# Batched attention with a gated expert layer: narrowing v on GpSimd, block sums over 128 rows, a new rule for the constant products, weights and last rows in pieces

## The chip, the cores and the metric

The kernel runs on one core of a Trainium2 chip. The metric is the device time of one execution in microseconds. Every set of runs measured the kernel before beside the tested kernel on the same chip. Each run also lists its span (first to last instruction) and the mean clock that TensorE was granted. On one core a run is called slow when it is more than 1.5% above the fastest run of the same kernel.

## The reference, cut to what matters

```python
B, H, S, D = 4, 8, 768, 64          # q, k, v: fp32
k_sum = k.reshape(B, H, 24, 32, D).max(axis=3)     # one key per block of 32
v_sum = v.reshape(B, H, 24, 32, D).mean(axis=3)    # block sums of v (scaled)
# scores: 31 neighbours (|i-j| < 16) plus the 24 block keys, softmax, times [v, v_sum]
x = attn.transpose(0, 2, 1, 3).reshape(B, S, 512)
pooled = x.mean(axis=1)                            # the gate needs the whole batch
e_idx = argmax(pooled @ w_gate)                    # one of 8 experts per batch
out = gate_w * (relu(x @ w1[e_idx]) @ w2[e_idx])   # w1: 512x1024, w2: 1024x512
```

Two things follow for timing. The gate of a batch can only be computed when its attention is complete. And w1 and w2 (1 MB each in bf16, 2 MB as stored) cannot be loaded before the gate has named the expert.

## The kernel before: the parts that matter here

A list scheduler (class `Sched`) places every operation on its engine before the program is emitted. Where it thinks TensorE too idle, it inserts constant products, which compute nothing but keep TensorE active.

```python
SPAN = 3.0; DENSE = 0.47; FILL_TO = 50.0
def keep_warm(self, t, op):
    ...
    past = sum((e - max(s, t - self.SPAN)) * d for s, e, d in self.work[-40:] if ...)
    thin = self.DENSE * self.SPAN - past - n * unit
    if t > 7.0 and thin > 0:
        more = min(int(thin / unit) + 1, 10)
```

v arrives in fp32 in `v_f`. It is cast to bf16 straight into the place where the value products read it, in two halves of 64 rows. The block sums are products of those 64-row halves with a 0/1 selector `bind`: twelve for each of batches 1 to 3, and twelve smaller ones for each of the four pairs of heads in batch 0.

```python
def cast_v(b, c, eng):
    for odd in range(2):
        dst = vblks[b % 2][0:QB, c, odd:NJ:2, :, 0:D]
        src = v_f[odd * QB : (odd + 1) * QB, :, 2 * c : 2 * c + 2, :]
        ...
for j in range(NJ):                                   # NJ = 12
    nc.tensor.matmul(out_ps[p0 : p0 + 32, 0 : n * D], lhsT=bind[:, j, :],
                     rhs=vblks[b % 2][0:QB, ps, j, :, 0:D], ...)
```

w1 is loaded in two halves in batch 0 and whole in the others, on GpSimd's queue, behind the gate:

```python
def w1f(half):
    fs = slice(half * (F // 2), (half + 1) * (F // 2)) if b == 0 else slice(0, F)
    nc.gpsimd.dma_start(sb["w1"][:, :, fs], moe_w1[ds(sb["e"], 1)]...[:, :, fs])
```

The softmax here doesn't subtract the row's maximum and nothing guards it: scores larger than these inputs give would overflow.

## Time and profile before

| what | before |
|---|---|
| median of 3 runs | 183.13 us (181.32 to 185.94) |
| profiled run | 182.19 us, span 180.6, mean clock 0.941 |
| TensorE / VectorE / ScalarE / GpSimd busy | 95% / 57% / 61% / 27% |
| batch 0's gate (L839, first) | 43.81 us |
| first product of w1, batch 0 | 53.55 us |
| batch 3's gate | 143.52 us |
| TensorE at half clock | 22.72 to 43.2 us |

I divide the span into four stretches at three events that each kernel has: from the start to gate 0, from there to the first product with w1, from there to gate 3, and from there to the end. Before: 43.81, 9.74, 89.97 and 37.08 us. TensorE is nearly full, so what counts in each stretch is what TensorE has to do, at which clock, and what it waits for. The lines are shown in the prediction.

### The profile page before, as it was taken

How to read it: one execution, taken by the hardware profiler on the slowest of the kernel's cores; microseconds unless marked ns; L12 is line 12 of the kernel's file. 1: busy time of each engine (PE TensorE's matmuls, PEld its weight loads, DVE VectorE, ACT ScalarE, POOL GpSimd, SP SyncE). 2: the span in 40 equal slices, each digit the busy share in tenths (PEclk: the TensorE clock that was granted, in tenths of full speed). 3: DMA queues.
4: the chain of work that ended last, by engine and by line, in shares of the span. 5: the costliest groups of instructions: out<-in, count | busy, mean ns of one | idle time of the engine just before them, and what ended most of it. 6: DMA issues, size and time to landing. Idle time of an engine off the chain costs nothing.

```text
span 180.6 us, 4939 instructions
## 1 busy us (share of the span) xinstructions
PE 170.7 (95%) x2083; PEld 96.2 (53%) x2083; DVE 103.2 (57%) x240; ACT 110.3 (61%) x201; POOL 48.5 (27%) x70
## 2 busy tenths in 40 slices
PE   6988899999999999799999999999999999999991
PEld 2454756665646566354665654555575544465440
DVE  5899966546978766849893944089986200000000
ACT  3085244575887799244788873967899733377241
POOL 6999651000781160671026003000000030000000
PEclk9999955557999999999999999999999999999999
DMA  5999999705499999999999941999700049990063
GB/s 103 202 234 176 191 247 210 129 4 75 57 206 178 210 243 203 149 202 245 231 255 247 282 80 58 173 249 263 158 4 5 0 78 240 268 230 0 3 231 116
DMA packets 21590, 29.06 MB, mean 161 GB/s; under 512 B 3744, under 2 KB 15008, under 8 KB 21568
## 3 DMA queue, kind: packets, MB, share of 16 engines
q0 software_dynamic: 15184, 20.58, 64.4%
q1 hardware_dynamic: 6384, 8.17, 14.9%
q8 instruction: 16, 0.26, 0.6%
q14 instruction: 6, 0.05, 0.1%
HBM read 35.67 MB, written 6.29 MB: 232 GB/s over the span
## 4 chain that ended last, share of the span: by engine, by line
PE 63%; DMA 18%; DVE 10%; issue 3%; ACT 1%; POOL 1%; POOLq 1%; ACTq 0%; DVEq 0%
PE hps L949 12%; PE hps L980 12%; DMA q_nat<-in_q_dram 9%; PE third L949 6%; PE third L980 6%; DMA w_sb<-in_moe_w_dram 6%; DMA v_f<-in_v_dram 4%; PE sc L607 4%; PE ops L461 3%; PE ops L645 3%; PE tps L681 3%; PE third L1068 3%; DVE vblk L363 3%; PE kps L526 3%; PE tps L552 2%
## 5 line engine op out<-in xcount | busy, mean ns | idle before, releaser
L618 ACT ACTIVATE aT<-sc 128x768 bf16<-128x768 f32 x32 | 25.9, 810 | 14.4 <-PE sc L607 14.3
L949 PE MATMUL hps<-xT_b,w_sb 128*128 128x512 bf16 (+1 forms) x172 | 33.1, 328 | 0.4 <-DMA w_sb<-in_moe_w_dram 0.4
L262 POOL DMA_DIRECT2D v_f<-in_v_dram x30 | 25.2, 851 | 26.6 <-DMA w_sb<-in_moe_w_dram 11.6
L949 PEld LDWEIGHTS <-w_sb 128*128 128x128 bf16 x256 | 22.8, 98 | 14.2 <-DMA w_sb<-in_moe_w_dram 0.8
L980 PE MATMUL hps<-w_sb,hT_sb 128*128 128x512 bf16 x128 | 29.8, 380 | 0.0
L980 PEld LDWEIGHTS <-hT_sb 128*128 128x128 bf16 x192 | 17.8, 98 | 19.9
L1068 PE MATMUL third<-idle_in 128*128 128x512 bf16 (+2 forms) x79 | 22.4, 421 | 1.9 <-DVE warm L275 1.6
L960 ACT ACTIVATE hT_sb<-hps 128x512 bf16<-128x512 f32 (+1 forms) x43 | 20.6, 493 | 4.9 <-PE hps L949 4.7
L870 POOL DMA_DIRECT2D w_sb<-in_moe_w_dram x5 | 3.8, 760 | 70.4 <-PE third L980 32.6
L990 ACT ACTIVATE o_sb<-hps,gcol 128x512 f32<-128x512 f32 x16 | 11.0, 688 | 11.7 <-PE hps L980 8.3
L622 DVE TENSOR_TENSOR aT<-aT,mask 120x768 bf16<-120x768 bf16 x28 | 15.5, 556 | 3.0 <-ACT aT L618 2.6
L949 PE MATMUL third<-xT_b,w_sb 128*128 128x256 bf16 (+1 forms) x84 | 17.0, 325 | 0.0
L671 DVE TENSOR_TENSOR xs<-ops,rv 128x384 bf16<-128x384 f32 x28 | 15.6, 558 | 1.0
L546 DVE COPY kT<-kps 128x960 bf16<-128x960 bf16 (+1 forms) x20 | 14.1, 745 | 2.3 <-PE kps L526 2.3
L689 ACT ACTIVATE xT_b<-tps 128x768 bf16<-128x768 bf16 x16 | 12.9, 808 | 4.0 <-PE tps L681 3.9
L980 PE MATMUL third<-w_sb,hT_sb 128*128 128x512 bf16 x64 | 15.2, 380 | 0.0
L363 DVE CAST vblk<-v_f 64x768 bf16<-64x768 f32 x22 | 13.2, 601 | 2.4 <-issue 2.1
L1068 PEld LDWEIGHTS <-idle_in 128*128 128x128 bf16 x79 | 7.6, 111 | 11.9 <-issue 5.8
L645 PEld LDWEIGHTS <-aT 120*64 120x64 bf16 (+1 forms) x384 | 9.6, 119 | 7.9 <-issue 3.4
L461 PE MATMUL ops<-vblk,bind 64*32 64x128 bf16 (+1 forms) x84 | 12.0, 286 | 1.5 <-DVE vs L475 0.9
L990 ACT ACTIVATE o_sb<-third,gcol 128x512 f32<-128x512 f32 x8 | 5.5, 688 | 12.2 <-PE third L980 9.2
L361 ACT ACTIVATE vblk<-v_f 64x768 bf16<-64x768 f32 x10 | 8.5, 846 | 6.6 <-DMA v_f<-in_v_dram 6.6
(75 smaller groups left out, 207.1 us busy)
## 6 DMA issues: line engine op xcount, KB each, us to landing
w_sb<-in_moe_w_dram POOLq DMA_DIRECT2D x7, 1024.0 KB, 13.3
out_dram<-o_sb SPq DMA_DIRECT2D x24, 256.0 KB, 6.0
v_f<-in_v_dram POOLq DMA_DIRECT2D x30, 192.0 KB, 9.7
k_nat<-in_k_dram POOLq DMA_DIRECT2D x6, 384.0 KB, 8.9
q_nat<-in_q_dram POOLq DMA_DIRECT2D x6, 384.0 KB, 10.0
vblk<-vblk SPq DMA_DIRECT2D x12, 89.4 KB, 6.5
w_sb<-in_moe_w_dram POOLq DMA_DIRECT2D x2, 512.0 KB, 7.2
k_nat<-in_k_dram POOLq DMA_DIRECT2D x4, 192.0 KB, 4.5
```

Source lines behind the costliest of these rows:

```text
L262: eng.dma_start(v_f[:, :, h, :], v[b, h].rearrange("(j p) d -> p j d", p=128))
L363: eng.tensor_copy(dst, src)
L461: nc.tensor.matmul(out_ps[p0 : p0 + 32, 0 : n * D], lhsT=bind[:, j, :], rhs=vblks[b % 2][0:QB, ps, j, :, 0:D], start=(j == 0), stop=(j == ...
L618: nc.scalar.activation(aT, sb["sc"][:, :, 0 : NH * QB], ACT.Exp, scale=SCALE)
L622: nc.vector.tensor_tensor(out=aT[0:NR], in0=aT[0:NR], in1=mask[:, hf * NH : (hf + 1) * NH, :] .rearrange("p j c -> p (j c)") .unsqueeze(1) ...
L645: nc.tensor.matmul(ops[(j % 2) * QB : (j % 2 + 1) * QB, hh, jj // 2, :], lhsT=aT[0:rows, hh, jj * QB : (jj + 1) * QB], rhs=vb[0:rows, pr, ...
L671: nc.vector.tensor_tensor(out=sb["xs"][pr][:, hf * NS : (hf + 1) * NS, :, :].rearrange("p s h d -> p h s d"), in0=ops[:, :, :, 0:D], in1=r ...
L949: nc.tensor.matmul(ps["t"][:, 0 : c1 - c0], lhsT=sb["w1"][:, dt, ft * 128 : (ft + 1) * 128], rhs=sb["xT"][:, dt, c0:c1], start=(dt == 0), ...
L960: nc.scalar.activation(sb["hT"][:, ft, c0:c1], ps["t"][:, 0 : c1 - c0], ACT.Relu)
L980: nc.tensor.matmul(ps["t"], lhsT=sb["hT"][:, ft, st * 128 : (st + 1) * 128], rhs=sb["w2"][:, ft, :], start=(ft == 0), stop=(ft == NFT - 1),)
L990: nc.scalar.activation(ps["o"], ps["t"], ACT.Copy, scale=sb["gcol"][:, 0:1])
L1068: nc.tensor.matmul(idle[:, 0:c], lhsT=idle_in[:, 0:128], rhs=idle_in[:, 0:c], start=True, stop=True)
```

## The change

The intent is fourfold. Constant products follow a new rule of the scheduler: each kind of product gets a weight, and the scheduler asks for a mean of 1.05 over 3.4 us (`DENSE`, `SPAN`). These are numbers of the program. For batches 1 to 3, GpSimd narrows v to bf16 (`v_h`), so that VectorE's and ScalarE's copies into place read bf16 and the fp32 buffer comes free early. The block sums read `v_h` in 128 rows, six products instead of twelve. w1 comes in four pieces in batch 0 and in two in batch 3, and the last 128 output rows in two halves of columns. The tables that assign work to engines and the priorities were retuned with it.

```diff
-    DENSE = 0.47
+    DENSE = 1.05
...
-            thin = self.DENSE * self.SPAN - past - n * unit
+            thin = self.DENSE * self.SPAN - past - 2.5 * n * unit
...
-    CAST = ("DADD", "DDAD", "ADDD", "ADDA")
-    MK = ("DDPP", "DDDD", "DDDD", "DDDD")
+    CAST = ("AADA", "DDAD", "ADDD", "AADA")
+    CHUNKS = (4, 1, 1, 2)
+    MK = ("DDPP", "DDDD", "DDDD", "PDDD")
...
-            src = v_f[odd * QB : (odd + 1) * QB, :, 2 * c : 2 * c + 2, :]
+            src = (v_hs[b % 2] if b else v_f)[odd * QB : (odd + 1) * QB, :, 2 * c : 2 * c + 2, :]
...
+        for c in range(NP * (b > 0)):
+            narrow.append(add("POOL", 0.8, [loads[2 * c], loads[2 * c + 1]] + v_h_free.get(b - 2, []),
+                lambda b=b, hs=hs: nc.gpsimd.tensor_copy(v_hs[b % 2][:, :, hs, :], v_f[:, :, hs, :])))
...
+                for j in range(NH * (b > 0)):             # NH = 6
+                    nc.tensor.matmul(out_ps[p0 : p0 + 32, 0 : n * D], lhsT=bind2[:, j, :],
+                                     rhs=v_hs[b % 2][:, j, :, :], ...)
...
-            fs = slice(half * (F // 2), (half + 1) * (F // 2)) if b == 0 else slice(0, F)
+            fs = slice(c * F // CHUNKS[b], (c + 1) * F // CHUNKS[b])
...
+        return [o_st(st) for st in range(NST - 1)] + [
+            o_st(NST - 1, 0, DM // 2), o_st(NST - 1, DM // 2, DM) ]
```

(The list is cut; weights of single products, priorities and engine tables are left out.)

## The prediction

> **What bounds the kernel now.** I read the page first, then the timeline of TensorE, the busy time in short stretches, the chain and the groups. From the page:
>
> ```profile
> PE   6988899999999999799999999999999999999991
> DVE  5899966546978766849893944089986200000000
> PEclk9999955557999999999999999999999999999999
> DMA  5999999705499999999999941999700049990063
> ```
>
> TensorE is full nearly everywhere, so its own work sets the time, except in two places. First, slices 5 to 9 (22.6 to 45 us) run at half clock, with the DMA idle at the end: all loads are in, and the next weights wait for batch 0's gate (the expert's index). In stretches of one microsecond:
>
> ```profile
> 22.00:23.00 1.00, 1.00 (x43) 0.91 (x38) 0.99 (x1) 0.66 (x1) 0.59 (x1) 0.86 1.22 247
> 23.00:24.00 1.00, 1.00 (x17) 0.59 (x13) 1.00 (x3) 0.15 (x1) 0.24 (x1) 0.50 1.14 272
> ...
> 43.00:44.00 1.00, 1.00 (x12) 0.41 (x10) 0.00 (x0) 1.00 (x3) 0.00 (x0) 0.90 0.93 134
> ```
>
> The figure before the last two is the clock: it falls at about 22.72 us (0.86 = 0.72 x 1 + 0.28 x 0.5) and comes back near 43.2. What lay before each change, in the timeline (start, us, instructions):
>
> ```profile
> 19.09 0.39 PE L1068 MATMUL third<-idle_in 128*128 128x512 bf16 x1
> 20.05 0.86 PE L461 MATMUL ops<-vblk,bind 64*32 64x128 bf16 x12 [0.57 <-DVE vs L475]
> ...
> 39.44 2.00 PE L1068 MATMUL third<-idle_in 128*128 128x512 bf16 x5
> 41.23 0.85 PE L681 MATMUL tps<-identb,xs 128*128 128x128 bf16 x6
> 41.87 2.02 PE L1068 MATMUL third<-idle_in 128*128 128x512 bf16 x6
> 43.81 0.35 PE L839 MATMUL ops<-wg_sb,pooled 128*1 128x8 f32 x8
> ```
>
> L1068 are the constant products that only keep TensorE active. One of them in 3.5 us was too few; eleven in a row brought the clock back. L839, at 43.81, is batch 0's gate. The second place is the end:
>
> ```profile
> 153.26 2.21 PE L1068 MATMUL third<-idle_in 128*128 128x512 bf16 x10 [0.24 <-ACT o_sb L990]
> 155.86 1.90 PE L949 MATMUL hps<-xT_b,w_sb 128*128 128x512 bf16 x8 [0.39 <-DMA w_sb<-in_moe_w_dram]
> ```
>
> Batch 3's w1 was issued at 145.79 and landed 10.03 us later (the chain); TensorE ran out of batch 2's products at 153.02, so 2.84 us are lost. Between, TensorE idles little: 1.15 us at 73.5, where the gate's reciprocal sits on VectorE behind casts waiting for v.
>
> [...] The trace has no such copy; its selects on GpSimd took 287 ns for 128 columns and 591 for 384, 1.19 ns a column, so about 1.05 us for 768. [...] casts took 0.79 us while GpSimd issued loads (16.4 to 19.7) and 0.56 when it was idle (40.3).
>
> **The change part by part.**
>
> *Constant products.* The weights of the new rule, applied to the old trace with the windows laid from 22.72 backwards, give mean activities of 1.30, 1.58, 1.33 and then 0.86 (19.31 to 22.72) against the threshold of 1.05: it picks the window that lost the clock. The cold windows have 1.1 to 1.3, until 2.41 in the one that regained it. The compiled order shows for the changed kernel 38 units of 128 columns (18 and 20) around the second and third blocks' transposes, plus 13 before the last query transpose of batch 0. If the clock stays full, what ends batch 0's attention? In the 20.5 slow us TensorE's work is 10.3 at full clock, of which 3.1 are constant products, so VectorE, ScalarE and hand-offs take over. Adding VectorE's compiled instructions up to the gate at their old durations gives about 28 us (memsets 3.9, masks 2.3, key copies, maxima and query copies 8, normalisations 8 x 0.75, masks on scores 4 x 0.56, block sums 4 x 0.3, one pair of casts 1.2, three of batch 1 at 0.6, second memsets 1.6), start 1.1, so 29. It also gets lighter: two of three batch 0 pairs of casts go to ScalarE (2 x 1.2), which had 1 to 2 of 5 us busy there. With waits between score blocks (0.65 product + 0.81 exponential + two hand-offs, 1.8 us each, four in a row from about 20, then 5 us to the gate) I put the gate at 34 instead of 43.8.
> The loads limit this too: they keep the DMA full until 32 in the old trace, the narrowing of batch 1 needs v (landed near 30), and four copies (4.2 us) plus the new selector (two selects, 0.8) stand on GpSimd's queue before the gate's loads. So w1 goes out at about 36.5 instead of 46.3. Landing in quarters, its first products can start after some 5 us, at 41.5; TensorE's own list between gate and that point is about 6.9 us, the same time. Before: 53.5. Gain 12.0, of which 1.4 is the block sum of batch 1 and 0.6 two score products that move later.
>
> *Block sums.* From the groups:
>
> ```profile
> L461 PE MATMUL ops<-vblk,bind 64*32 64x512 bf16 x36 | 8.4, 378 | 0.0
> L363 DVE CAST vblk<-v_f 64x768 bf16<-64x768 f32 x22 | 13.2, 601 | 2.4 <-issue 2.1
> ```
>
> Twelve take 2.73 us in the chain, six of 128 rows half: 1.37 saved for each of batches 2 and 3, on the bound engine: 2.7.
>
> *Narrowing.* [...] v's buffer is free after GpSimd, not after the casts. Worth only the 1.15 us wait, half of which I count: 0.6.
>
> *Moved.* Batch 3's first pair masks by products: four of 384 columns, 0.32 to 0.38 us each at half clock (L596), so about 0.16 here: +0.6. The 0.6 of score products comes back.
>
> *End.* w1 in halves: 512 KB landed in 7.2 us (median of batch 0), so the first half is there 7.2 after issue instead of 10.0, when TensorE finishes its list: gain 2.8, less 0.5 because the output tiles of batch 2 still wait for stores (2.2 us twice on ScalarE). w2 landed near 162.4, 18.9 after the gate; needed 20 after it, so it just fits. Last rows in halves: the final eviction is 0.3 shorter, the store half as large: 0.5.
>
> Sum: 12.0 + 2.7 + 0.6 + 2.3 + 0.5 - 0.6 - 0.6 = 16.9 at best: span 180.6 to 163.7. The old profiled run is 182.2 us for that span, 1.6 more: 165.3.
>
> **The rivals.** (1) The clock falls in the changed kernel too. Its order from the last query transpose of batch 0 to the last value product has only three constant units. At full-clock durations of the trace times the rule's weights it holds four masked score blocks (0.60 us x 1.1), seven value products (0.58 x 0.66), three transposes of x (0.36 x 2.0), two transposes (0.46 x 1.35) and 0.4: 9.1 in all, from 8.6 us of TensorE. The hand-offs above stretch it to 11 to 13 us, which makes 0.70 to 0.83, under the 0.86 of the window that lost the clock. [...] I give this six chances in ten. It would come later than before (near 25) and meet less work: of the 17.9 us that the slow stretch from 25.98 to the gate takes now, half remains, 9 or so at half clock, so the gate comes at 37 to 38: 4 us back, 169.3. (2) The DMA becomes the bound. It is full from 46.3 to 106 in the old trace and moves earlier only by 9.8, while TensorE moves by 12 and more: stalls of 2 to 3 us before batch 2. Against it: some 12 us of idle DMA remain before and after. 168. (3) GpSimd is slow [...]: batch b's gate loads stand behind the copies of v of b+1, so w1 would come 3 to 4 us late three times. TensorE has 15 us of other products after gates 1 and 2, so mainly gate 0 pays: 169. (4) The clock part fails wholly: only 2.7 + 1.4 + 2.3 + 0.5 stay, 176.
>
> **Range and chances.** 165.3 plus 0.6 x 4 for rival 1, and some 1.3 for the lesser chances of rivals 2 and 3, gives 169.0 us. Low 163.5 is the sum with a fast state; high 176.5 is rival 4. The old three runs spread from 181.3 to 185.9[...]. Over 2% faster means under 179.5: all rivals but two at once give that, so 0.95; within 2% 0.04; slower 0.01.
>
> **What would show it.** Right: PEclk 9 in all slices of batch 0, or at most two of half clock; L839 first at 33 to 36; first product of w1 near 42; block sums of later batches 1.36 us; copies on GpSimd about 1.05 us; no constant products near the end, and under 1 us idle there. Wrong: half clock for 15 us or more; gates' loads on GpSimd waiting for narrowing; TensorE idle on w1 in the middle.

## The result, and the profile after

The changed kernel took 169.62 us (median of four runs, 168.70 to 171.37), the kernel before beside it 182.22 us. The ratio is 0.941, with a 95% interval of 0.923 to 0.959. Here and below, a ratio is the mean time of one kernel's fast runs over that of the other's of the same rounds, so it is not quite the ratio of the medians.

The profiled run is the slowest of the four: 171.37 us, span 169.8, clock 0.98, called slow. The page of the changed kernel, in 40 slices of 4.2 us:

```profile
PE   6989999799999997699999999999999999899992
DVE  5987985867997756977965746649754210000000
PEclk9999999969999999879999999999999999999999
DMA  4999999954999999699999989999200039994143
```

The five slices at half clock have become parts of three: in slice 8, and in slices 16 and 17. The DMA's hole, at slice 8 in both, is smaller. Stretches of one microsecond give the edges (the clock is the third figure from the right):

```profile
32.00:33.00 1.00, 0.92 (x26) 0.81 (x26) 0.61 (x2) 0.99 (x2) 0.00 (x0) 1.00 1.27 202
33.00:34.00 1.00, 0.93 (x3) 0.37 (x3) 0.84 (x4) 0.20 (x1) 0.91 (x2) 0.66 1.23 214
...
36.00:37.00 1.00, 1.00 (x4) 0.40 (x3) 0.23 (x1) 0.43 (x2) 0.00 (x0) 0.64 0.73 106
37.00:38.00 1.00, 1.00 (x34) 0.73 (x33) 0.36 (x4) 0.00 (x0) 0.00 (x0) 1.00 0.55 86
```

0.66 = 0.31 x 1 + 0.69 x 0.5: half clock from 33.31 to 36.72, for 3.41 us. A second such stretch lies at 70.86 to 74.27, also 3.41 us and 37.55 after the first, 11.0 times its length; the one of the kernel before (22.72 to 43.20, 20.48 us) is 6.0 times as long. Below, a window is a stretch of 3.41 us. In TensorE's timeline around the first (start, us, instructions, idle before):

```profile
30.59 0.35 PE L675 MATMUL ops<-vblk,aT 96*64 96x65 bf16 x10
31.81 0.22 PE L675 MATMUL ops<-vblk,aT 96*64 96x65 bf16 x2 [0.86 <-issue]
...
33.07 1.67 PE L1106 MATMUL third<-idle_in 128*128 128x512 bf16 x4 [0.16 <-issue]
34.54 0.85 PE L711 MATMUL tps<-identb,xs 128*128 128x128 bf16 x6
35.17 2.12 PE L1106 MATMUL third<-idle_in 128*128 128x512 bf16 x6
37.23 0.34 PE L869 MATMUL ops<-wg_sb,pooled 128*1 128x8 f32 x8
```

L675 are value products, L711 the transposes of x, L1106 the constant products, L869 the gate: at 37.23 instead of 43.81. Something new stands in the first lines: TensorE stops for 0.86 us in the middle of a group of twelve, waiting for nothing that the profile records ("issue"). Batch 1's gate is the second new thing. The timeline of all engines:

```profile
67.27 0.83 POOL L445 CAST v_h<-v_f 128x768 bf16<-128x768 f32 x1 [1.47 <-DMA v_f<-in_v_dram]
68.13 0.73 DVE L371 COPY vblk<-v_h 64x768 bf16<-64x768 bf16 x2 [1.18 <-POOL v_h L445]
68.50 0.75 POOL L899 DMA_DIRECT2D w_sb<-in_moe_w_dram  x1 [0.40 <-issue]
...
69.21 0.09 DVE L919 RECIPROCAL grec<-se 1x1 f32<-1x1 f32 x1
...
69.36 0.38 PE L922 MATMUL ops<-grec,ones_row 1*128 1x1 f32 x2 [1.26 <-DVE grec L919]
```

Read it backwards. TensorE waits 1.26 us for the gate's reciprocal. The reciprocal waits in VectorE's queue behind a copy into place (L371), that copy waits for GpSimd's narrowing (L445), and the narrowing waits for v to land. The load of w1 (L899) stands on GpSimd behind the same narrowing.

The end, where 2.84 us were lost before, now reads:

```profile
144.65 1.03 PE L980 MATMUL hps<-xT_b,w_sb 128*128 128x512 bf16 x4
145.51 0.60 PE L980 MATMUL third<-xT_b,w_sb 128*128 128x256 bf16 x4
146.64 1.02 PE L980 MATMUL third<-xT_b,w_sb 128*128 128x512 bf16 x4 [0.52 <-ACT hT_sb L991]
```

No constant products, 0.52 us of idle. And the groups of the parts that were exchanged:

```profile
L445 POOL CAST v_h<-v_f 128x768 bf16<-128x768 f32 x12 | 10.0, 831 | 8.5 <-DMA v_f<-in_v_dram 7.5 <-ACT hT_sb L991 1.0
...
L371 DVE COPY vblk<-v_h 64x768 bf16<-64x768 bf16 x14 | 5.8, 414 | 4.0 <-POOL v_h L445 3.8
L479 PE MATMUL ops<-v_h,bind 128*32 128x512 bf16 x18 | 5.4, 447 | 0.0
```

On average a narrowing takes 0.83 us and a copy into place 0.41 (before 0.60), and 18 sum products stand where 36 stood. The unaltered changed kernel was profiled twice more as a control, below. The last of these profiles is fast (169.49 us, span 167.9, clock 0.998), so it is the better partner of the profile of before. That one was fast in its own set of three, but it lies 2.0% above a later run beside it (178.68), and its clock of 0.941 is among the lower ones. By stretch, in us:

| kernel (profile) | to gate 0 | to first w1 product | to gate 3 | to the end | span |
|---|---|---|---|---|---|
| before | 43.81 | 9.74 | 89.97 | 37.08 | 180.6 |
| changed, first profile (clock 0.98) | 37.23 | 7.29 | 90.80 | 34.48 | 169.8 |
| changed, last control (clock 0.998) | 35.70 | 7.33 | 90.70 | 34.17 | 167.9 |

Batch 0 gave 9.0 to 10.5 us and the end 2.6 to 2.9. The middle, in which the block sums were halved, gave nothing: it is 0.7 to 0.8 us longer. That is what the experiments have to explain.

The runs also say how much of the gain goes with the clock. Three runs of the kernel before had a mean clock of 0.977 to 0.979 and took 176.57 to 177.68 us (mean 177.1). Seven runs of the changed kernel had 0.978 to 0.980 and took 171.09 to 173.66 us (mean 171.9). So about 5 of the 12.6 us between the medians remain at an equal mean clock; the rest goes with the clock. This is a comparison of runs and not a test.

### The profile page after: what moved, and what is told of

Its sections match the earlier page's. It is cut to its first block, busy times and chain, and to the rows that moved or that the text cites. A ratio compares the mean times of both kernels' runs of the same rounds, so it can differ in the third digit from the quotient of the medians.

```text
span 169.8 us, 4877 instructions
## 1 busy us (share of the span) xinstructions
PE 158.6 (93%) x2038; PEld 91.8 (54%) x2065; DVE 97.2 (57%) x232; ACT 112.1 (66%) x205; POOL 61.7 (36%) x87
## 4 chain that ended last, share of the span: by engine, by line
PE 69%; DMA 13%; POOL 8%; issue 4%; ACT 2%; DVE 1%; POOLq 1%; ACTq 0%
PE hps L1013 15%; PE hps L980 13%; PE third L1013 8%; DMA w_sb<-in_moe_w_dram 8%; PE third L980 6%; DMA v_f<-in_v_dram 5%; PE third L1106 4%; PE sc L637 4%; PE ops L675 3%; PE tps L711 3%; POOL v_f L263 3%; PE kps L556 3%; PE ops L479 2%; PE tps L582 2%; PE ops L487 2%
## 5 line engine op out<-in xcount | busy, mean ns | idle before, releaser
L980 PE MATMUL hps<-xT_b,w_sb 128*128 128x256 bf16 (+1 forms) x165 | 32.7, 326 | 0.6 <-issue 0.2
L1013 PE MATMUL hps<-w_sb,hT_sb 128*128 128x512 bf16 (+1 forms) x120 | 28.2, 373 | 0.5 <-issue 0.2
L899 POOL DMA_DIRECT2D w_sb<-in_moe_w_dram x8 | 6.0, 753 | 40.8 <-DVE grec L919 39.8
L1106 PE MATMUL third<-idle_in 128*128 128x512 bf16 (+3 forms) x61 | 18.8, 424 | 2.1 <-DVE warm L277 1.7
L1023 ACT ACTIVATE o_sb<-hps,gcol 128x512 f32<-128x512 f32 (+1 forms) x16 | 10.8, 674 | 10.0 <-PE hps L1013 6.6
L1013 PE MATMUL third<-w_sb,hT_sb 128*128 128x512 bf16 (+1 forms) x69 | 15.7, 367 | 0.3 <-issue 0.2
L1023 ACT ACTIVATE o_sb<-third,gcol 128x512 f32<-128x512 f32 (+1 forms) x9 | 6.0, 663 | 11.3 <-PE third L1013 4.6
L675 PEld LDWEIGHTS <-aT 120*64 120x64 bf16 (+1 forms) x384 | 8.7, 111 | 8.6 <-issue 3.7
L445 POOL CAST v_h<-v_f 128x768 bf16<-128x768 f32 x12 | 10.0, 831 | 8.5 <-DMA v_f<-in_v_dram 7.5
L700 DVE RECIPROCAL rv<-ops 128x6 f32<-128x6 f32 x28 | 5.4, 193 | 12.6 <-PE ops L675 10.2
L1106 PEld LDWEIGHTS <-idle_in 128*128 128x128 bf16 x67 | 6.6, 111 | 9.7 <-issue 4.1
L675 PE MATMUL ops<-vblk,aT 120*64 120x65 bf16 (+1 forms) x336 | 10.8, 199 | 0.9 <-issue 0.9
```

The lines of the kernel that those rows point to most:

```text
L675: nc.tensor.matmul(ops[(j % 2) * QB : (j % 2 + 1) * QB, hh, jj // 2, :], lhsT=aT[0:rows, hh, jj * QB : (jj + 1) * QB], rhs=vb[0:rows, pr, ...
L980: nc.tensor.matmul(ps["t"][:, 0 : c1 - c0], lhsT=sb["w1"][:, dt, ft * 128 : (ft + 1) * 128], rhs=sb["xT"][:, dt, c0:c1], start=(dt == 0), ...
L1013: nc.tensor.matmul(ps["t"][:, 0:n], lhsT=sb["hT"][:, ft, st * 128 : (st + 1) * 128], rhs=sb["w2"][:, ft, c0:c1], start=(ft == 0), stop=(ft ...
L1023: nc.scalar.activation(ps["o"][:, 0:n], ps["t"][:, 0:n], ACT.Copy, scale=sb["gcol"][:, 0:1])
L1106: nc.tensor.matmul(idle[:, 0:c], lhsT=idle_in[:, 0:128], rhs=idle_in[:, 0:c], start=True, stop=True)
```

## The experiments

My theory after the result had four parts. (a) The constant products hold the clock in batch 0, and with it most of the gain. (b) w1 in halves gives the 2.6 to 2.9 us at the end. (c) The shorter block sums save TensorE work in the middle, but waits at the gates take it back, and these waits come from the order of queues in front of a v that has not landed. (d) The "issue" stall is TensorE waiting for instructions. The rivals were: the new order of work and not the constant products; the loads themselves; some cause in the stalled group itself.

### Control: the changed kernel again (e0_after, e11_after_again)

No edit.

> The changed kernel again, as a control of the other runs of this call and to see it without the dips of the clock. Theory (two windows of half clock cost it something in most runs): time 168.5 to 171.5, ratio to before 0.925 to 0.945, and runs differ by whole windows: a run at clock 1.00 is about 1 to 3 us shorter than one at 0.98. Rival (the dips cost nothing since TensorE was waiting anyway): time does not go with the granted clock.

> Control: the changed kernel, unaltered. 168.5 to 172.5 us, about 0.945 of the kernel before; one to three half-clock windows.

Measured: 171.76 us (170.00 to 173.66, ratio 0.951) and 170.62 us (169.49 to 172.05), beside 182.09 and 181.53 of the kernel before. The first control's profile had half-clock windows at 33 and 67 us, the second's none before its last microsecond. So the same program loses the clock in batch 0 in two profiles of three; why the third kept it is not shown. What is compared below is compared with the control where there was one, or by stretches.

### Constant products alone, added to the kernel before (e1_before_fill, e1b_again)

```diff
+        fills[0] += 1
+        if fills[0] == 7:
+            n = 24            # was 4 units, near 19 us
```

> The kernel before, same order, one block of constant products near 19 us made 24 units instead of 4 (1.1 us more of TensorE work). Theory (the half clock from 22.7 to 43.2 was caused by that one thin window): the clock stays full past 23, falls at most once later in batch 0 for one to three windows, gate of batch 0 at 37 to 40 instead of 43.8, time 4 to 6 us shorter (ratio 0.967 to 0.978). Rival (the stretch is bound by VectorE and hand-offs, the clock is a symptom): ratio 0.99 to 1.01.

> The kernel before with the larger block of constant products once more, for a second profile: its first profile was its fastest run (180.46), and its others went up to 189.94. If the clock alone makes the difference, a profile of 184 us or more shows five or more half-clock windows (mean clock under 0.95) and a TensorE stall with no wait of about 1.8 us as in the first. If the supply of instructions does, that stall is over 3 us or there are several, at a similar clock. A profile under 182 us tells nothing new.

Measured: 184.74 us (180.46 to 189.94), ratio 1.022, and in the second call one run at 182.52, its state unknown. My expectation of 4 to 6 us faster was missed. The clock did stay: the profiles lose it at about 30.8 and 30.1 us instead of 22.72, and have three and four windows of half clock instead of six. But gate 0 came at 42.01 and 43.97, against 43.81, and the first w1 product at 51.74 and 53.70. In its place TensorE stalled, for 1.81 us in the first profile and, in the second:

```profile
28.87 0.22 PE L645 MATMUL ops<-vblk,aT 96*64 96x65 bf16 x2 [2.32 <-issue]
```

So in these two profiles the clock kept from 22.7 to 30 us brought gate 0 forward by 1.8 us or not at all, with a stall of 1.8 and 2.3 us in the way (what the traces show of it stands below, under the place of the stall). That the clock is worth nothing in the old order does not follow: of the 33 runs of the kernel before, the three with the highest mean clock (0.977 to 0.979) took 176.57 to 177.68 us and the eight with the lowest (0.930 to 0.933) 182.91 to 184.38. Where those three kept the clock isn't known, since none was profiled. Some runs of this kernel were slower than the kernel before at an equal mean clock (188.04 at 0.936). Neither profile fell on such a run, so their cause stays open.

### The changed kernel without three blocks of constant products (e2_after_nofill)

```diff
+        fills[0] += 1
+        if fills[0] in (7, 9, 10):
+            return True       # leaves out blocks of 18, 20 and 13 units
```

> The changed kernel, same order, without the three blocks of constant products between 15 and 22 us (18, 20 and 13 units). Theory (these blocks hold the clock): half clock from about 20 to 23 on and until the last constant blocks before the gate, 4 or more windows; gate of batch 0 at 40 to 43 instead of 37.2; time 3 to 6 us longer than the changed kernel of this call. Rival (the schedule, not the blocks, made batch 0 shorter): within 1 us of the changed kernel, as the missing 2.8 us of products even make room.

Measured: 177.00 us (175.78 to 177.73), ratio 0.983, 5.2 us over the control. Its page:

```profile
PEclk9999555556999999978999999999999999999999
```

Half clock from about 18.3 to 42.2 (seven windows, one more than before), gate 0 at 42.97, first w1 product at 50.26. With the order kept, these three blocks are worth 5.2 us. The new order without them leaves gate 0 nearly where it was (0.8 us earlier), and in the first test more constant products without the new order did so too, there with the stall in the way. Together they bring it forward by 6.6 to 8.1 us. The new rule mostly moved the constant products: before gate 0 the kernel before has 56 of them, the control 57, and this kernel 43. From the gate to the first w1 product it took 7.29 us, as in the changed kernel, so the 2.4 us between the gate and w1 are independent of the clock. TensorE idles 0.0 to 0.1 us there in both kernels, so its list got shorter; the halved sums of batch 1 are 1.3 of it (2.80 to 1.47 us). The quarters of w1, which have to land in time for that (the first at 42.98 in the last control, used at 43.03), were not tested alone.

### Block sums computed twice (e3_sums_twice)

```diff
-                for j in range(NH * (b > 0)):
+                for i in range(2 * NH * (b > 0)):
+                    j = i % NH
```

> The changed kernel, same order, with the six products of 128 rows of the block sums of batches 1 to 3 issued twice (the second round overwrites the first): the old TensorE cost, 2.7 us each. Theory (TensorE is the bound in all three places): 4.1 us longer, 3.3 to 4.6. Rival (batches 2 and 3 sit in waits for v and for weights): 1.4 to 2.5 us longer.

Measured: 173.26 us (171.25 to 175.33), 1.5 us over the control, by medians and by the means of the fast runs. The six products take 1.47 us at full clock, so some 4.4 us of TensorE work were added in the three batches and a third of it came out as time. The rest filled waits. This was what the rival said; my theory said 4.1. The runs of both spread by some 4 us, so 1.5 is known to about 1 us either way, and 4.1 is excluded. By stretch, the sums of batch 1 cost 1.3 (8.59 us from gate 0 to w1 instead of 7.3, without idle time), while in the middle TensorE's idle time fell to 1.69 us from the 3.65 of the first control: there the added work went into waits.

### w1 of batch 3 whole (e4_w1_whole)

```diff
         def w1f(c):
+            if b + 1 == B:
+                if c: return
+                fs = slice(0, F)
```

> The changed kernel, same order on TensorE, with batch 3's w1 loaded in one piece instead of two halves. Theory of the prediction (the first half lands 2.8 us before the whole): TensorE idle 2 to 3 us before the first product of batch 3's w1, time 2.0 to 2.8 us longer than the changed kernel, whose six runs of the last call had a median of 171.8. Rival (the stores of batch 2 hold the output tiles and would have stopped TensorE there anyway): 0 to 0.7 us longer.

Measured: 174.75 us (173.71 to 181.10), ratio 0.981. It was run on another chip. The last stretch of its profile is 37.04 us, against 34.48 and 34.17 in the changed kernel and 37.08 before, and the others are those of the changed kernel. The wait is back:

```profile
148.04 1.04 PE L984 MATMUL hps<-xT_b,w_sb 128*128 128x512 bf16 x4 [2.68 <-DMA w_sb<-in_moe_w_dram]
```

So the halves of w1 give 2.6 to 2.9 us, the whole gain of the last stretch. The halves of the last rows, which this kernel still has, were not tested alone; with w1 whole the last stretch is only 0.04 us shorter than before, so nothing is left for them on balance.

### More constant products (e8_dense13)

```diff
-    DENSE = 1.05
+    DENSE = 1.3
```

> The changed kernel with the rule's threshold at 1.3 instead of 1.05, so some 20 more units of constant products in batch 0's attention (order elsewhere shifts a little). Theory (window 29.9 to 33.3 lost the clock at 0.92): clock full through batch 0 in most runs, gate of batch 0 about 0.9 us earlier or the same, time 1 us shorter to 0.5 longer. Rival (TensorE's stall of 0.9 to 2.1 us near 31 to 33, where nothing that the profile shows is waited for, empties the window whatever is added): half clock stays, time up to 1.5 us longer.

Measured: 175.64 us (171.35 to 176.18), ratio 0.968, where at most 0.5 us over the changed kernel was expected. Its profile keeps the clock through batch 0, and still gate 0 comes at 38.56, 2.9 us later than in the control that kept the clock too, and gate 3 at 140.16. Before gate 0 it has 16.9 us of constant products, the control 14.8, so some 2.1 of the 2.9 us are the added ones themselves. (The higher threshold also shifted the order a little.)

### The place of the stall (e9_shift24)

```diff
+        shifts[0] += 1
+        for _ in range(12 * (shifts[0] == 1)):     # 12 tiny products, 24 instructions
+            nc.tensor.matmul(idle[:, 0:4], lhsT=idle_in[:, 0:128], rhs=idle_in[:, 0:4], ...)
```

> The changed kernel with 12 more tiny products (24 TensorE instructions) in the first block of constant products, where TensorE only waits. In three different programs TensorE stalled 0.8 to 2.1 us between the 956th and the 958th of its instructions. Theory (the stall is the supply of instructions[...]): it stays at the same count, so it falls 24 instructions earlier in the work: inside the six transposes of x (after four of them) instead of inside the twelve value products. Rival (the value products wait for something): it stays between the tenth and eleventh value product. Time within 1 us of the changed kernel.

In the changed kernel and its variants with the stall, it falls at instruction 957 of TensorE's recorded order (954 in the first profile, where some records are missing), before the eleventh value product of one group. In both profiles of the test of constant products above it falls at 701, in another head's group. That is not the place that the expectation names for three programs, but it is exactly 256 instructions earlier.

Measured: 172.26 us (169.66 to 173.78), no clear change. The timeline:

```profile
31.50 0.54 PE L711 MATMUL tps<-identb,xs 128*128 128x128 bf16 x6
31.97 0.38 PE L675 MATMUL ops<-vblk,aT 96*64 96x65 bf16 x12
```

The group that had stalled now runs through, twelve in a piece. The stall did not reappear at the new place 956, which is inside the six transposes at 31.50; they took 0.54 us instead of 0.51. TensorE got there at about 31.8, and in the changed kernel and its controls the stalls had ended at 31.81, 33.22 and 31.96. That fits something that arrives at about the same time in each, but the stall moving, which the expectation asked for, was not seen.

The kept traces add to this. They hold the DMA packets of kind "instruction" on queue 8, 16 packets of 16 KB in each kernel, for the 4,100 to 4,180 recorded instructions of TensorE, so one for 256 to 261 of them if all are TensorE's. Ten of the fourteen profiles have a stall with no recorded wait, 0.55 to 2.32 us long, at instruction 957 or 701. In all ten it ends 1.41 to 1.65 us after such a packet has landed: 30.22 and 31.81 in the first profile of the changed kernel, 31.66 and 33.22 in the first control, 27.46 and 28.87 in the second profile of constant products alone. The kernels that came to the place later than that did not stall: this one at 31.75 with its packet landed at 30.30, the one with more constant products at 32.86 with 30.56. The packets are not labelled by engine, and no profile records what TensorE waited for. That it waited for instructions is my reading of these places and times; it fits all of them.

### The copies into place from fp32 (e6_cast_f32)

```diff
-            src = (v_hs[b % 2] if b else v_f)[odd * QB : (odd + 1) * QB, ...]
+            src = v_f[odd * QB : (odd + 1) * QB, ...]
```

> The changed kernel, but the copies into place read v in fp32 as in the kernel before; the narrowed v feeds the block sums alone. VectorE's copies then take 0.56 to 0.60 us instead of 0.41, about 2 us more over the twelve of batches 1 to 3, and v's buffer is held until they are done. If the narrowing is worth what the prediction gave it (0.6) or nothing, the time is within 1.5 us of the control's; the copies no longer stand behind GpSimd, so the wait at gate 1 may even shrink. If the lighter copies and the early freeing of v's buffer carry the change, it is slower by over 2 us.

Measured: 172.31 us (170.42 to 174.41) against 170.62 of the control; the means of the fast runs are 171.15 and 170.33. The group in its profile:

```profile
L371 DVE CAST vblk<-v_f 64x768 bf16<-64x768 f32 x16 | 11.2, 702 | 2.2 <-DMA v_f<-in_v_dram 1.7 <-issue 0.3
```

In the control the fourteen copies took 5.6 us and the two casts of batch 0 1.3, so VectorE does 4.3 us more here, and the time rises by 0.8 (fast runs) to 1.7 us (medians). The runs of the two kernels spread by 4.0 and 2.6 us, so that isn't clear of noise: the narrowing as a feed of VectorE may be worth some 1 us, and the over 2 us of the one expectation did not come. TensorE's wait at gate 1 did not shrink (2.23 us, against 1.01 and 1.16 in two pieces in the control). The two engines also got in each other's way: casts of this kernel that started during a narrowing took 0.79 to 1.09 us, all but one of the others 0.55 to 0.57, and the two narrowings that began beside a cast (62.61 and 97.11) took 1.20 us each, where those of the changed kernel take 0.83 on average.

### The gates ahead of the copies (e7_gate_first, e10_gates_first)

The first of these puts the third and fourth copy of batch 2's v behind gate 1's reciprocal on VectorE. The second does it for batch 3 and gate 2 too (there the fourth copy is on ScalarE), and moves the narrowing of these pieces behind the loads of w1 and w2 on GpSimd.

```diff
+                    after=[order_pool[-1]] if b > 1 and c > 1 else [],      # narrowing; second only
...
+                    after=[grec_done[0]] if b > 1 and c > 1 else [],        # copies; first: b == 2
```

> The changed kernel with two of batch 2's casts ordered on VectorE and ScalarE behind the reciprocal of gate 1, so that the gate no longer waits for the loads of v. Theory (TensorE's idle 0.96 and 1.26 us at gate 1, and the window of half clock after it, come from VectorE's queue standing behind v): no half clock near 71 to 74, idle at gate 1 under 1.2 us in all, 1.0 to 3.0 us shorter than the changed kernel. Rival (the loads themselves are the bound there, v and the weights arrive no earlier): within 0.7 us, the wait only moves to the block sums or the first products of w1.

> The changed kernel, with the third and fourth pairs of v of batches 2 and 3 narrowed behind the issue of w1 and w2 of the gate before (gates 1 and 2) and copied into place on VectorE behind that gate's reciprocal. In the run with only batch 2's copies moved, gate 1's w1 went out at 65.89 instead of 68.50 and gate 2 came at 92.09 instead of 97.30, but then VectorE stood 4.85 us behind batch 3's narrowing and w1 went out at 99.70, 7.6 us after its gate, so only 1.1 us was left. If it is the order of the queues (engines in order, standing behind a v that has not landed) that holds the middle, w1 of batch 2 goes out near 95 here, and the time is 2 to 5 us under the control's. If it is the loads themselves (DMA full from 46 to 97), w1 goes out earlier but lands no earlier, and TensorE waits elsewhere: within 1.5 us of the control, or slower, because batch 3's v comes later.

Measured: 172.76 us (170.23 to 175.50, ratio 0.966) for the first, so nothing clear. Its profile shows why. Gate 1's wait for the reciprocal is gone: w1 went out at 65.89 instead of 68.50 us, gate 2 came at 92.09 instead of 97.30 (66.95 and 94.19 in the last control, which kept the clock as this profile did until then). Then the same trap caught batch 3:

```profile
98.14 0.35 PE L639 MATMUL sc<-qT,kT 64*128 64x64 bf16 x12 [2.65 <-DVE qT L597]
```

The copy of queries stood on VectorE behind a copy into place that waited for v. For the second kernel: 168.97 us (167.66 to 169.21) against 170.62 (169.49 to 172.05) of the control, a ratio of the fast runs of 168.63 / 170.33 = 0.990, the fastest kernel. By the spread of these runs the 1.7 us are known to about 1 us either way. All six runs are fast, with clocks of 0.99 and 1.00; the control's are 0.98 to 0.998. Gate 2 in the control:

```profile
94.19 0.35 PE L869 MATMUL ops<-wg_sb,pooled 128*1 128x8 f32 x8
...
97.42 0.73 DVE L371 COPY vblk<-v_h 64x768 bf16<-64x768 bf16 x2 [2.91 <-POOL v_h L445]
...
99.05 0.35 PE L637 MATMUL sc<-qT,kT 64*128 64x64 bf16 x12 [1.45 <-DVE qT L595]
...
99.77 0.75 POOL L899 DMA_DIRECT2D w_sb<-in_moe_w_dram  x1 [0.43 <-PE sc L637]
```

and in the reordered kernel:

```profile
94.56 0.35 PE L872 MATMUL ops<-wg_sb,pooled 128*1 128x8 f32 x8
...
96.86 0.75 POOL L902 DMA_DIRECT2D w_sb<-in_moe_w_dram  x1 [0.43 <-PE third L984]
```

From the gate to the load of w1 it now takes 2.3 us instead of 5.6, and TensorE's wait is gone. But w1 landed no earlier (110.16 us, 109.06 in the control), and its first product in both came 2 to 4 us after that, so the gain is the wait that went, and not the earlier load. The middle stretch of three kernels, before, control and reordered (stretch, its length, TensorE busy, and so on):

```profile
53.55:143.52 89.97, 88.47 (x1217) 50.42 (x1212) 62.88 (x140) 65.95 (x124) 17.58 (x23) 1.00 0.86 174
```

```profile
43.03:133.73 90.70, 86.90 (x1230) 50.42 (x1228) 63.18 (x140) 67.96 (x128) 28.28 (x36) 1.00 0.92 179
```

```profile
43.92:133.09 89.17, 87.05 (x1232) 50.64 (x1228) 62.95 (x141) 67.73 (x128) 28.45 (x36) 1.00 0.94 182
```

The first figure minus the second is TensorE's idle time: 1.50 us before, 3.80 in the control, 2.12 in the reordered kernel. So the change did take work off TensorE in the middle (88.47 to 86.90, at full clock in both), and waits took 2.3 us. In the control they are 1.01 and 1.16 us at gate 1 and 1.45 at gate 2. Part of these came from the order in the queues, since another order removed 1.7 of them. The gain in time, 1.7 us, lies between what the queue theory (2 to 5) and the rival that the loads bind (under 1.5) had said, nearer to the latter. A part of it did not come from this stretch: the two profiled runs are only 0.28 us apart, because the reordered kernel took 1.4 us longer from gate 0 to the first w1 product (8.69 against 7.33). There it met the same trap at gate 0, which the edit had left alone: batch 1's last narrowing ended at 34.88 us instead of 33.67, VectorE stood 1.40 us for it, and TensorE then idled 1.20. The shifted kernel above lost 0.98 us in the same way (8.46 from gate 0 to w1). Over all runs the steadier clock may add to the gain.

## Why the prediction was right or wrong

The predicted time, 169.0 us, is 0.6 under the measured median, and all four first runs lie in the range. But it is a sum of a best case and of chances, so each term has to be looked at. The best case was a span of 163.7, which splits by the text's own numbers into a first w1 product at 41.5, a middle of 87.9 (89.97 - 2.7 - 0.6 + 0.6 + 0.6) and an end of 34.3 (37.08 - 2.3 - 0.5). The last control, which kept the clock, had 43.03, 90.70 and 34.17. The misses are 1.5, 2.8 and -0.1, and make the whole difference between 163.7 and 167.9.

**Constant products and gate 0: the mechanism right, the best case 1.7 us too early.** The gate came at 35.70 with the clock kept; the text had put it at 34 from VectorE's list. Part of that is the "issue" stall (0.98 us in that profile), which the prediction didn't have. The prediction counted the clock as the cause and lighter engines as an addition. The runs support the clock (5.2 us with the order kept). The new order alone moved gate 0 by only 0.8 us, and the test of constant products alone doesn't say what the clock is worth without that order, because the stall came in its place.

**Rival 1, six chances in ten: it came in two of three profiles, later and in smaller size.** The text had the clock fall near 25 us and stay low for some 9; the one lost window lies at 33.3 to 36.7, after the stretch that the text had named as thin. The gate came at 37.23, inside the 37 to 38 that the text gave for this case, which is partly luck: a shorter loss was added to a later best case. The other such profile had 38.45, with a stall of 2.11 us. The cost was 1.5 to 2.8 us and not 4. The scheduler's threshold of 1.05 agrees here: its weights applied to the trace of the changed kernel, with the windows laid from 33.31 backwards, give about 0.8 for the window that lost the clock and 1.0 to 1.1 for the two before it. TensorE's busy time alone does not tell which windows lose the clock: after 2.39 of 3.41 us busy (29.90 to 33.31) and 2.03 (67.45 to 70.86) in the changed kernel, and 2.84 (19.31 to 22.72) in the kernel before, it was lost, while after 2.46 (64.03 to 67.45) it was kept. The rule's weights give these four about 0.8, 0.8, 0.9 and 1.2. One reading of the prediction does not come out so: by these weights the first half-clock window of the kernel before (22.72 to 26.13), with 1.57 us of constant products in it, has about 1.6 and not 1.1 to 1.3, so being over the threshold was not enough to regain the clock there.

**Between gate 0 and w1: right where nothing waited.** 7.3 us in the three profiles of the changed kernel, 9.74 before; the prediction had 41.5 - 34 = 7.5. In the shifted and the reordered kernel it took 8.46 and 8.69, for the wait described above.

**Block sums: the size of the work right, its place on the path wrong.** Six take 1.47 us where 1.36 was expected, and TensorE's work in the middle did fall. The step that failed is "on the bound engine: 2.7". TensorE was busy, but at gates 1 and 2 it stood for VectorE and ScalarE, and there saved work becomes longer waiting: 2.3 of it. The doubled sums cost 1.5 us instead of 4. Batch 1's sums, counted with gate 0, did give their 1.3 us.

**Narrowing: the step "Worth only the 1.15 us wait, half of which I count: 0.6" had the wrong sign for the wait.** The feed itself was worth 0.8 to 1.7 us in the test from fp32, not clear of noise. But the wait at gate 1 grew from 1.15 us to 0.96 and 1.26 in the first profile (1.01 and 1.16 in the control), where the copies into place on VectorE and ScalarE wait for GpSimd and it waits for v. That the narrowing made it grow is not shown, since without its feed the wait was 2.23 us. Batch 2's v had wholly landed 2.8 us after gate 1 before (73.20 and 70.41) and 2.9 after it now (67.22 and 64.36), so v came forward only as far as the gate did. In the first profile the thin stretch before it also lost the clock, 70.86 to 74.27. Rival 3 had looked for this at gate 0, where in the first profile the narrowing ended well before the gate (33.92, gate 37.23), though in the shifted and reordered kernels it did not and cost 1.0 to 1.2 us; and it had taken gates 1 and 2 for harmless because TensorE had 15 us of other products. It had, but the gate's reciprocal and the next batch's query copy stood in VectorE's queue behind the blocked copy.

**Rival 2, the DMA: not shown as the bound of the middle, and not excluded as part of it.** The narrowing waits 7.5 us in all for v. With the gates ahead of it, on nearly the same loads, the middle got 1.5 us shorter. Yet w1 of batch 2, sent out 2.9 us earlier, landed 1.1 later.

**End: the sum right, the terms not.** 2.6 to 2.9 measured against 2.3 + 0.5, and w1 in halves gives nearly all of it. So the 0.5 taken off for stores of batch 2 was not lost, and the 0.5 for the last rows did not come on balance; that they cancel is luck.

**Duration of single operations.** A narrowing took 0.83 us, where 1.05 was estimated from the selects of the kernel before (287 ns for 128 columns, 591 for 384). A copy into place from bf16 took 0.36 us in the median, a cast from fp32 in the kernel before 0.56. The mean of 0.41 comes from three of the fourteen copies, which started while GpSimd worked: 0.93 us for one during a narrowing, 0.43 and 0.51 during the selects for `bind2`, against 0.35 to 0.36 for the others. The prediction had noted the same of casts beside GpSimd's load issues (0.79 us against 0.56). Why VectorE takes longer there is not shown.

The central value was right because the allowance of 3.7 us for rivals 1, 2 and 3 was near the 4.2 to 6.1 us by which the best case was too short in the two profiles. Clock windows in batch 0 and waits behind the narrowing were both named, the latter at the wrong gate; the "issue" stall was not. That the sizes add up so closely is in part luck.

## What to carry to other kernels

Work taken off a busy engine gives time only where that engine isn't waiting at a hand-off, so subtract busy from length for each stretch before counting a saving: here 1.6 us of work went and 2.3 us of waiting came. Put what a later stage hangs on, such as a gate's small instructions, ahead of copies whose data is still on its way, on every engine that they share (here 1.7 us, known to about 1). Constant products to hold a clock have to be enough and no more: here the three blocks were worth 5.2 us, and 2.1 us more of them came out as later time. An engine that gets faster can meet new limits: here TensorE stalled for 0.55 to 2.32 us in ten of fourteen profiles, with no recorded wait.
